# Pooled attention and a soft mixture of experts in one launch: the PE transposes of the weights leave the score banks for the bank of D^T P, by pairs of tiles

## The chip, the cores and the metric

The kernel runs on one core of one Trainium2 chip, in one launch. The metric is device time in microseconds (us), from the first to the last instruction of the program on that core and the little that lies around it. TensorE is called PE below, its weight load PEld, VectorE DVE, ScalarE ACT, GpSimd POOL, and SyncE, which issues most DMAs, SP.

## The reference, cut to what matters

```python
# attention: B=4, C=128, 12288 queries of each batch, 768 pooled keys (= values)
kv_pool = kv.reshape(B, H // 4, 4, W // 4, 4, C).mean(axis=(2, 4))
k = v = kv_pool.reshape(B, -1, C) @ w_sr
s = (q @ k.transpose(0, 2, 1)) / sqrt(C)
a = exp(s - s.max(-1)); a /= a.sum(-1) + 1e-09
x = (a @ v).reshape(B * 12288, C)
# soft MoE over all 49152 rows: 8 experts with 4 slots each = 32 columns
logits = x @ phi
d = softmax over the rows of logits;   slot_input = d.T @ x
slot_out = per expert: relu(slot_input @ w1) @ w2
c = softmax over the 32 columns of logits
return c @ slot_out
```

All inputs and the output are float32.

## The kernel before, in words

The 49152 rows are 384 tiles of 128 queries (96 tiles for each of the four batches). The program never forms x. For a tile it forms the unnormalised weights p = exp(s - max), 128 x 768, and uses them twice: the logits are p @ (v phi), divided by the row sums, and the slots need D^T P, that is (weights of the second softmax)^T @ p, which is summed over a batch and multiplied by v at the batch's end.

**A tile's steps.** `qk` (L353): six matmuls of 384 columns, for an exact product of values split into two parts, into a score tile of two PSUM banks. `top` (L357, L359): DVE's row maximum and its shift. `exp` (L369): ACT's exponential from the score tile to p in SBUF; its accumulator output, a row sum for each query, goes to a column of `SUMS`. p must then be transposed, because the logits contract over the 768 keys. Four of its six blocks of 128 keys go through the DMA: `hi` (L376, ACT) and `lo` (L379, POOL) split them into two fp16 parts, and `turn` (L384, SP) issues a transposing DMA into `pt`. The other two blocks go through PE: `tp` (L391) makes two PE transposes and `tev` (L402) is the DVE copy of the result to `pf` in SBUF. In this kernel the transposes of tile i are written to columns 384 to 511 of the two banks of the score tile of tile i+2 (`AHEAD = 2`), whose scores take columns 0 to 383 of each bank, and each tile has its own 256-column copy.

**A group's steps.** Eight tiles are a group (47 such groups, and two of four tiles at the end). `lmm` (L418) forms the group's logits from `pf` (fp32) and `pt` (fp16) in the bank `L`; `lt_out` (ACT), `lt_turn` (PE, L443), `recip` (L451, L453: the row sums plus eps, and the reciprocal), `logits`, `colmax`, `cross` (PE, L483), `newmax`, `below`, `weights` (ACT, L505) and `scaled` (L518, gives `dp`) carry the running softmax over the rows. `total_mm` (L524) and `ymm` (L541, 8 matmuls of 192 columns for a pair of tiles as the order prints them, each run as two entries of the trace: 64 for a group) accumulate the group's sum and D^T P in the bank `DB`, columns 0 to 191 and 192; `total` (L532) adds into `EA`, and `yacc` (L551) into `acc`. The row sums of the groups, `SUMS`, are columns 208 to 231 of the same bank `DB`.

**PSUM.** Eight banks: three score tiles (ring `s`) of two banks, one bank `L`, one bank `DB`. Instructions of different engines that touch one bank of a tile are made to wait for each other by semaphores even where their columns differ (two reads too); the rows of the profile that the prediction quotes show such waits.

**Order.** The program is written by a list scheduler (class `Plan`): each step is an `op` with an engine, an estimated duration, a latency, a priority, the steps that it depends on, and the rings that it takes (`acq`) or uses (`use`). `emit` picks by estimated start time and priority, and what it picks is the order of the instructions on each engine's queue; the engines then run their queues in order, each instruction waiting on its semaphores. So the numbers in `dve`, `act`, `pool` and in the `op` calls set the order and nothing else. Rings: 3 score tiles, 11 pairs of p (`p32`), 6 `hl`, 6 `pt`, 5 pairs of `pf`, one `L`, one `D`. SP carries, in order, the loads of q, the transposing DMAs and the loads of the next batch's kv, which POOL adds up (L253).

After the last tile comes the tail: the experts, the second softmax's weights c (transposed on PE into `L` and `DB` by turns, L896), and the product with the slots' outputs (L917), copied by DVE and ACT and sent out.

Of the kernel before, what the change touches and what calls it, by code (L numbers as in the profile page):

```python
# [122 lines left out]
def attention_then_soft_moe(ctx: ExitStack, tc: tile.TileContext, qT, kv0, kvT, w_sr, w_srT, phi, w1, w2, outT):  # L123
# [34 lines left out]

    KD = 4
    KP = NT - KD  # L160
    AHEAD = 2

    RINGS = {"p32": 11, "hl": 6, "pt": 6, "pf": 5, "e": 2, "q": 3, "qs": 2, "s": 3, "L": 1, "D": 1, "dp": 2, "lt": 1, "kT": 2, "U": 2, "V": 1, "kv": 1}
    plan = Plan(RINGS)
# [196 lines left out]
    def exp(i):  # L361
        g = GOF[i]
        if i == groups[g][0]:
            o = 208 + GMAX * (g % 3)
            SUMS[g] = DB[:, o : o + GMAX]
        if i % 2 == 0:
            P32[i // 2] = ring("p32", [P, 2, NK], F32, f"p_{i // 2}")
        t = i - groups[g][0]
        nc.scalar.activation(  # L369
            P32[i // 2][:, i % 2, :].rearrange("p (h k) -> p h k", h=2), S[i][:, :, :HK], AF.Exp, bias=NM.pop(i), scale=1.0,  # L370
            accum_out=SUMS[g][:, t : t + 1],
        )

# [9 lines left out]
            PT[i // 2] = ring("pt", [P, 2, 2 * KD, P], F16, f"pt_{i // 2}")  # L383
        nc.sync.dma_start_transpose(out=PT[i // 2][:, i % 2], in_=HL.pop(i).rearrange("p a k -> p (a k)"))  # L384

    def tp(i):
        if i + AHEAD >= NTL:
            S[i + AHEAD] = sslot(f"t_{i}")
        for x in range(KP):
            k = KD + x  # L390
            nc.tensor.transpose(  # L391
                out=S[i + AHEAD][:, x, HK : HK + P], in_=P32[i // 2][:, i % 2, k * P : (k + 1) * P], identity=ident
            )

    def tev(i):
        if i % 2 == 0:
            PF[i // 2] = ring("pf", [P, KP, 2, P], F32, f"pf_{i // 2}")
        dst, src = PF[i // 2][:, :, i % 2, :], S[i + AHEAD][:, :, HK : HK + P]
        if TEV(i) == "ACT":
            nc.scalar.activation(dst, src, AF.Copy)  # L400
        else:
            nc.vector.tensor_copy(dst, src)  # L402

# [185 lines left out]


    def dve(n):
        return n / 960 + 0.09

    def act(n, aps=0):
        return n / 1200 + 0.1 + 0.093 * aps

    def pool(n):
        return 0.1 + n * 1.93e-3  # L600

    HEAD = 22.0
    PER = 2.0
# [1 line left out]

    def T(i):
        return HEAD + i * PER

    def TEV(i):
        return "DVE"  # L610

    pooled[0] = stage[:, KVC - 1, :]
    ops["q", 0] = op("ACT", 0.3, 9.0, -300, [], lambda: q_load(0), acq=[("q", 0)])
# [57 lines left out]
    def group_ops(g):  # L671
        s, n = groups[g]
        b = s // TPB
        first = s % TPB == 0
        base = T(s + n - 1) + 2.0
        lk = ("L", g)
        pts = [("pt", p) for p in range(s // 2, (s + n) // 2)]
        p32 = [("p32", p) for p in range(s // 2, (s + n) // 2)]
        pfs = [("pf", p) for p in range(s // 2, (s + n) // 2)]
        k = [0]  # L680

        def go(name, eng, cost, dep, fn, acq=(), use=(), lat=0.1, raw=0.12):
            k[0] += 1
            ops[name, g] = op(eng, cost, lat, base + 0.05 * k[0], dep, fn, acq=acq, use=use, raw=raw)
            return ops[name, g]

        turns = [ops["turn", i] for i in range(s, s + n)]
        mm = 4 * KD * max(0.0255, gt(g) * P / 9000)
        a = go("l0", "PE", 4 * KP * gt(g) * P / 2200, [ops["tev", i] for i in range(s, s + n)] + [ops["u", b]], lambda: lmm(g, 0),
               acq=[lk], use=pfs + [("U", b)], lat=0.17)  # L690
        for x in range(3):
            a = go(f"l{x + 1}", "PE", mm, [a] + (turns if x == 0 else []), lambda x=x: lmm(g, x + 1), use=[lk, ("U", b)] + pts, lat=0.17, raw=0.0)
        a = go("lt", "ACT", act(gt(g) * P, 1), [a], lambda: lt_out(g), acq=[("lt", g)], use=[lk])
        a1 = go("tt", "PE", 0.14 * gt(g), [a], lambda: lt_turn(g), use=[lk, ("lt", g)], lat=0.25)
        r = go("r", "DVE", 0.38, [a, ops["e", s + n - 1]], lambda: recip(g), use=[lk])
        a = go("ll", "DVE", dve(n * NS), [a1, r], lambda: logits(g), use=[lk])
        a = go("cm", "DVE", dve(n * NS) + 0.33, [a], lambda: colmax(g), use=[lk])
        a = go("cx", "PE", 0.27, [a], lambda: cross(g), use=[lk], lat=0.3)
        rc = go("rc", "DVE", 0.18, [r], lambda: rcopy(g), use=[lk])
        a = go("nm", "DVE", 0.55, [a, ops.get(("nm", g - 1))], lambda: newmax(g), use=[lk])  # L700
        sb = go("sb", "DVE", dve(n * NS), [a], lambda: below(g), use=[lk])
        w = go("w", "ACT", act(n * NS), [sb], lambda: weights(g), acq=[("e", g)], use=[lk])
        al = go("al", "ACT", 0.29, [a], lambda: decay(g)) if g else None
        d = go("dp", "DVE", dve(n * NS), [w, rc], lambda: scaled(g), acq=[("dp", g)], use=[lk, ("e", g)])
        t = go("tm", "PE", 0.14 * n / NQD, [w], lambda: total_mm(g), acq=[("D", g)], use=[("e", g)], lat=0.3)
        y = d
        for t0 in range(0, n, 2):
            y = go(f"y{t0}", "PE", 2 * 8 * 0.0425, [y, t], lambda t0=t0: ymm(g, t0, t0 + 2), use=[("dp", g), p32[t0 // 2], ("D", g)], lat=0.2, raw=0.0)
        ya = go("ya", "DVE", dve(NT * NS), [y, t, al, ops.get(("yt", b - 1)) if first else ops["ya", g - 1]], lambda: yacc(g), use=[("D", g)])
        go("to", "DVE", 0.16, [t, al, ops.get(("to", g - 1))], lambda: total(g), use=[("D", g)])  # L710
        rm = go("rm", "DVE", dve(n * NS), [sb], lambda: rowmax(g))
        rm = go("rs", "POOL", pool(n * NS), [rm], lambda: rowsub(g))
        ops["c", g] = go("re", "ACT", act(n * NS), [rm], lambda: rowexp(g))
        if (s + n) % TPB == 0:
            ty = go("ytu", "DVE", dve(NT * NS), [ya, ops.get(("sl", b - 1))], lambda: yturn(b))
            ops["yt", b] = ty
            sl = go("sl_", "PE", 0.27 * NT, [ty, ops["v", b]], lambda: slots(b), acq=[("D", ("s", b))], use=[("V", b)], lat=0.3)
            ops["sl", b] = sl
            m = go("ms", "DVE", 0.35, [ops["nm", g], ops.get(("sa", b - 1))], lambda: mstep(b, g), use=[lk])
            if b:  # L720
                m = go("me", "ACT", 0.2, [m], lambda: mexp(b))
            ops["sa", b] = go("sa_", "DVE", 0.35, [sl, m], lambda: sacc(b), use=[("D", ("s", b))])

    qn = 3
    for i in range(NTL):
# [3 lines left out]
        if i % TB == 0:  # L729
            if iq >= 1 and iq + 2 < NB:  # L730
                ops["q", iq + 2] = op("SP", 0.75, 2.0, t - 2, [ops["ql", iq - 1], ops["q", iq + 1]], lambda n=iq + 2: q_load(n), acq=[("q", iq + 2)])
            for n in ([0, 1] if iq == 0 else [iq + 1]):
                if n < NB:
                    a = op("ACT", act(BQ), 0.1, t - 2.0 if n else -50, [ops["q", n], ops.get(("ql", n - 1))], lambda n=n: q_hi(n), acq=[("qs", n)], use=[("q", n)])
                    ops["ql", n] = op("POOL", 1.31, 0.1, t - 1.0 if n else -50, [a], lambda n=n: q_lo(n), use=[("qs", n), ("q", n)])
        kd = [ops["k", b, 0], ops["k", b, 1]]
        ops["qk", i] = op("PE", 6 * 0.163, 0.17, t, [ops["ql", iq], ops.get(("qk", i - 1))] + kd, lambda i=i: qk(i), acq=[("s", i)], use=[("qs", iq), ("kT", b)], raw=0.0)
        a = op("DVE", dve(NK) + 0.1, 0.1, t + 1, [ops["qk", i]], lambda i=i: top(i), use=[("s", i)])
        ops["e", i] = op("ACT", 0.91 + 0.06, 0.1, t + 2, [a, ops.get(("e", i - 1))], lambda i=i: exp(i), acq=[("p32", i // 2)] if i % 2 == 0 else [],
                         use=[("s", i)] + ([("p32", i // 2)] if i % 2 else []))  # L740
        a = ops["hi", i] = op("ACT", act(KD * P), 0.1, t + 4, [ops["e", i], ops.get(("hi", i - 1))], lambda i=i: hi(i), acq=[("hl", i)], use=[("p32", i // 2)], raw=0.15)
        a = op("POOL", pool(KD * P), 0.1, t + 5, [a], lambda i=i: lo(i), use=[("hl", i), ("p32", i // 2)])
        ops["turn", i] = op("SP", 1.55, 2.2, t + 6, [a, ops.get(("turn", i - 1))], lambda i=i: turn(i), acq=[("pt", i // 2)] if i % 2 == 0 else [],
                            use=[("hl", i)] + ([("pt", i // 2)] if i % 2 else []))
        pend = [i - AHEAD] if i < NTL - 1 else [i - AHEAD + x for x in range(AHEAD + 1)]
        for x in pend:
            if x < 0:
                continue
            sk = ("s", x + AHEAD)
            late = x + AHEAD >= NTL  # L750
            a = op("PE", 0.135 * KP, 0.2, T(x) + 4.5, [ops["e", x], None if late else ops["qk", x + AHEAD]], lambda x=x: tp(x), acq=[sk] if late else [],
                   use=([] if late else [sk]) + [("p32", x // 2)], raw=0.0)
            ev = TEV(x)
            ops["tev", x] = op(ev, (act if ev == "ACT" else dve)(KP * P), 0.1, T(x) + 5.0, [a, ops.get(("tev", x - 1))], lambda x=x: tev(x),
                               acq=[("pf", x // 2)] if x % 2 == 0 else [], use=[sk] + ([("pf", x // 2)] if x % 2 else []))
            ops["tev_", x] = ops["tev", x]
        for x in pend:
            if x >= 0 and x == sum(groups[GOF[x]]) - 1:
                group_ops(GOF[x])
        ib = i % TPB  # L760
        if ib == 8 and b + 1 < B:
            nb = b + 1
# [285 lines left out]
```

## Time and profile before

| | |
|---|---|
| median of 3 runs | 1283.15 us (1279.59 to 1289.29) |
| the profiled execution, its own time | 1278.79 us |
| its span, first to last instruction | 1277.0 us |
| last `qk` of the program ends | 1144.1 us after the span's start |
| busy, of the span: PE / DVE / ACT / POOL | 77% / 65% / 60% / 54% |
| mean granted TensorE clock | 0.944 |

How to read it: the profile's page gives the busy time of each engine, the costliest groups of instructions (with the mean ns of one, the idle time of the engine just before them and who ended it), and the chain that ended last. The trace behind it also gives who waited for whom, the busy time of each engine in any stretch of the span, and the instructions in order of time. A PE entry's time runs from its start to its modelled end, so two neighbours can overlap; the step from one start to the next is what an instruction really takes of the engine.

### The profile page before, as it was taken

Reading aid. Unit: us, or ns where it says so; the run is one execution under the profiler, and the core shown is the slowest. Engines: PE = TensorE matmul, PEld = TensorE weight load, DVE = VectorE, ACT = ScalarE, POOL = GpSimd, SP = SyncE. Lnnn points to the kernel's source line nnn. Section 1 sums busy time; section 2 is a strip of 40 time slices with the busy share of each in tenths; the row PEclk is TensorE's granted clock in tenths of the full one; section 3 lists DMA queues with packets and bytes.
Section 4 is the critical chain, followed back from the end, with each engine's and each line's share of the span. In section 5 each row is a group of like instructions: output and inputs, shape, how many; then the busy total and the mean of one; then the engine's idle time right before and its main releaser. Section 6 shows DMA issues by size and latency. Waiting matters only on the chain. (4 is left out here: it accounts for less than half of the span.)

```text
span 1277.0 us, 27861 instructions
## 1 busy us (share of the span) xinstructions
PE 989.5 (77%) x10392; PEld 759.8 (60%) x10392; DVE 824.8 (65%) x2085; ACT 760.9 (60%) x1567; POOL 695.6 (54%) x584
## 2 busy tenths in 40 slices
PE   2787777778877877878878777887887787876876
PEld 2665666565666656656666666666665565654454
DVE  5665675666766756666766757656666666664675
ACT  1756675566666655666666656556576666661454
POOL 1576774454577864455487855455455555541231
PEclk9999999999999989999999999989999999996765
DMA  6688775555688765565688755466566565557477
GB/s 243 131 179 174 159 143 104 98 116 105 122 191 173 167 122 104 103 118 120 144 171 165 171 124 114 88 116 117 111 123 119 104 125 109 100 99 281 173 321 297
DMA packets 433016, 186.54 MB, mean 146 GB/s; under 512 B 408561, under 2 KB 410353, under 8 KB 432881
## 3 DMA queue, kind: packets, MB, share of 16 engines
q1 hardware_dynamic: 432304, 184.35, 65.3%
q8 instruction: 82, 1.34, 0.5%
q14 instruction: 54, 0.43, 0.1%
q10 hardware_dynamic: 576, 0.41, 0.1%
HBM read 58.87 MB, written 25.17 MB: 66 GB/s over the span
## 5 line engine op out<-in xcount | busy, mean ns | idle before, releaser
L379 POOL TENSOR_TENSOR hl<-p,hl 128x512 f16<-128x512 f32 x384 | 445.1, 1163 | 379.8 <-ACT hl L376 276.5
L369 ACT ACTIVATE p<-s,nm 128x768 f32<-128x768 f32 x384 | 345.8, 900 | 383.0 <-DVE pf L402 179.1
L353 PE MATMUL s<-kT,qs 128*128 128x384 f32 x2304 | 502.7, 355 | 0.4 <-DVE pf L402 0.3
L357 DVE TENSOR_REDUCE top<-s 128x1 f32<-128x768 f32 x384 | 365.2, 951 | 48.9 <-PE s L391 28.2
L353 PEld LDWEIGHTS s<-kT,qs 128*128 128x128 f32 x2304 | 390.2, 191 | 4.9 <-issue 3.4
L541 PE MATMUL DB<-p,dp 128*32 128x192 f32 x3072 | 168.8, 360 | 105.6 <-ACT p L369 96.5
L376 ACT ACTIVATE hl<-p 128x512 f16<-128x512 f32 x384 | 239.7, 629 | 8.5
L402 DVE COPY pf<-s 128x256 f32<-128x256 f32 x382 | 159.7, 418 | 98.3 <-ACT p L369 53.8
L391 PE MATMUL s<-ident,p 128*128 128x128 f32 x764 | 155.8, 285 | 82.8 <-ACT p L369 55.2
L541 PEld LDWEIGHTS DB<-p,dp 128*32 128x32 f32 x3072 | 94.0, 118 | 169.9 <-ACT p L369 123.4
L391 PEld LDWEIGHTS s<-ident,p 128*128 128x128 f32 x764 | 92.5, 144 | 144.6 <-ACT p L369 82.1
L343 POOL TENSOR_TENSOR qs<-q,qs 128x512 fp32r<-128x512 f32 x96 | 124.2, 1294 | 75.6 <-ACT qs L340 65.5
L551 DVE SCALAR_TENSOR_TENSOR acc<-acc,al,DB 128x192 f32<-128x192 f32 x45 | 18.6, 414 | 99.8 <-PE DB L541 68.3
L340 ACT ACTIVATE qs<-q 128x512 fp32r<-128x512 f32 x96 | 60.3, 629 | 22.9 <-PE s L353 12.2
L418 PE MATMUL L<-pt,u 128*32 128x256 f16 (+1 forms) x2352 | 74.0, 274 | 0.0
L253 POOL TENSOR_TENSOR LL<-LL 128x1536 f32<-128x1536 f32 x21 | 72.9, 3471 | 0.0
L359 DVE TENSOR_SCALAR nm<-top 128x1 f32<-128x1 f32 x384 | 59.1, 154 | 16.0 <-ACT p L369 0.5
L418 PEld LDWEIGHTS <-u 128*32 128x32 f16 x2352 | 59.7, 99 | 12.3 <-issue 10.7
L369 ACT ACTIVATION_READ_ACCUMULATOR p<-s,nm 128x1 f32 x384 | 63.3, 165 | 0.0
L889 POOL TENSOR_TENSOR LL<-LL,RM 128x512 f32<-128x512 f32 x24 | 24.9, 1049 | 69.5 <-DVE RM L884 69.5
L418 PE MATMUL L<-pf,us 128*32 128x256 f32 (+1 forms) x784 | 55.5, 390 | 0.7 <-DVE pf L402 0.4
L560 POOL TENSOR_TENSOR LL<-rm,LL 128x256 f32<-128x256 f32 (+1 forms) x49 | 29.9, 610 | 45.7 <-DVE rm L556 43.6
(118 smaller groups left out, 764.2 us busy)
## 6 DMA issues: line engine op xcount, KB each, us to landing
q<-qT SPq DMA_DIRECT2D x95, 256.0 KB, 2.9
outT<-o SPq DMA_DIRECT2D x30, 768.0 KB, 4.1
LL<-kvT SPq DMA_DIRECT2D x24, 768.0 KB, 5.0
kv<-kv SPq DMA_DIRECT2D x8, 768.0 KB, 9.9
pt<-hl SPq DMA_TRANSPOSE x384, 3.1
w<-w SPq DMA_DIRECT2D x7, 768.0 KB, 9.0
w<-w SPq DMA_DIRECT2D x11, 256.0 KB, 8.7
outT<-o SPq DMA_DIRECT2D x4, 384.0 KB, 3.9
```

Of the source, the lines that this page charges most:

```text
L253: nc.gpsimd.tensor_tensor(out=stage[:, 2:4, :], in0=stage[:, 2:4, :], in1=stage[:, 0:2, :], op=ALU.add)
L340: nc.scalar.activation(QSP[i][:, 0], QS[i], AF.Copy)
L343: nc.gpsimd.tensor_tensor(out=QSP[i][:, 1], in0=QS[i], in1=QSP[i][:, 0].bitcast(F32), op=ALU.subtract)
L353: nc.tensor.matmul(s[:, h, :HK], a, k[:, m, h * HK : (h + 1) * HK], start=(n == 0), stop=(n == 2))
L357: nc.vector.tensor_reduce(out=nm, in_=S[i][:, :, :HK], axis=XY, op=ALU.max, negate=True)
L369: nc.scalar.activation(P32[i // 2][:, i % 2, :].rearrange("p (h k) -> p h k", h=2), S[i][:, :, :HK], AF.Exp, bias=NM.pop(i), scale=1.0, ac ...
L376: nc.scalar.activation(HL[i][:, 0], P32[i // 2][:, i % 2, : KD * P], AF.Copy)
L379: nc.gpsimd.tensor_tensor(out=HL[i][:, 1], in0=P32[i // 2][:, i % 2, : KD * P], in1=HL[i][:, 0], op=ALU.subtract)
L391: nc.tensor.transpose(out=S[i + AHEAD][:, x, HK : HK + P], in_=P32[i // 2][:, i % 2, k * P : (k + 1) * P], identity=ident)
L402: nc.vector.tensor_copy(dst, src)
L418: nc.tensor.matmul(out.rearrange("p (h q) -> p h q", q=P) if gt(g) == 2 else out, lhs, rhs, start=start, stop=stop)
L541: nc.tensor.matmul(G[g]["D"][j * NS : (j + 1) * NS, : NT * NS].rearrange("p (k r) -> p k r", k=NT), G[g]["dp"][:, t, :], p[:, j], start=(t ...
```

## The change

The PE transposes of a pair of tiles (four, 512 columns) are written to the bank `DB`, as a step of their own that takes the ring `D`, which the group's `total_mm` and `ymm` take too. One DVE copy of 512 columns takes the place of two of 256. The row sums move from `DB` to an SBUF tile. `AHEAD` goes, and so do the score tiles that the last two tiles' transposes took. The priorities of the transposes (t+14) and of a group's steps (16 after its last tile's time) are set later, and the estimated durations of several steps are changed. Lines that only drop comments or blanks are left out; line numbers of the changed kernel are lower: L352 for `qk`, L356 for `top`, L367 for `exp`, L389 for `tp`, L393 for `tev`, L409 for `lmm`, L515 for `total_mm`, L523 for `total`, L532 for `ymm`, L540 and L542 for `yacc`.

```diff
     def exp(i):
         g = GOF[i]
         if i == groups[g][0]:
-            o = 208 + GMAX * (g % 3)
-            SUMS[g] = DB[:, o : o + GMAX]
+            SUMS[g] = wp.tile([P, GMAX], F32, tag="sums", name=f"sums_{g}", bufs=3)
...
-    def tp(i):
-        if i + AHEAD >= NTL:
-            S[i + AHEAD] = sslot(f"t_{i}")
+    def tp(u):
         for x in range(KP):
-            k = KD + x
-            nc.tensor.transpose(
-                out=S[i + AHEAD][:, x, HK : HK + P], in_=P32[i // 2][:, i % 2, k * P : (k + 1) * P], identity=ident
-            )
-
-    def tev(i):
-        if i % 2 == 0:
-            PF[i // 2] = ring("pf", [P, KP, 2, P], F32, f"pf_{i // 2}")
-        dst, src = PF[i // 2][:, :, i % 2, :], S[i + AHEAD][:, :, HK : HK + P]
-        if TEV(i) == "ACT":
-            nc.scalar.activation(dst, src, AF.Copy)
-        else:
-            nc.vector.tensor_copy(dst, src)
+            for h in range(2):
+                k = KD + x
+                o = (2 * x + h) * P
+                nc.tensor.transpose(out=DB[:, o : o + P], in_=P32[u][:, h, k * P : (k + 1) * P], identity=ident)
+
+    def tev(u):
+        PF[u] = ring("pf", [P, KP, 2, P], F32, f"pf_{u}")
+        nc.vector.tensor_copy(PF[u].rearrange("p x h q -> p (x h q)"), DB[:, : 2 * KP * P])
...
     def dve(n):
-        return n / 960 + 0.09
+        return n / 960 + 0.06
...
-        base = T(s + n - 1) + 2.0
+        base = T(s + n - 1) + 16
...
-        ops["qk", i] = op("PE", 6 * 0.163, 0.17, t, ...)
-        a = op("DVE", dve(NK) + 0.1, 0.1, t + 1, ...)
+        ops["qk", i] = op("PE", 6 * 0.166, 0.3, t, ...)
+        a = op("DVE", 1.08, 0.09, t + 1, ...)
...
-        pend = [i - AHEAD] if i < NTL - 1 else [i - AHEAD + x for x in range(AHEAD + 1)]
-        for x in pend:
...
-            sk = ("s", x + AHEAD)
-            late = x + AHEAD >= NTL
-            a = op("PE", 0.135 * KP, 0.2, T(x) + 4.5, [ops["e", x], None if late else ops["qk", x + AHEAD]], lambda x=x: tp(x), acq=[sk] if late else [],
-                   use=([] if late else [sk]) + [("p32", x // 2)], raw=0.0)
-            ev = TEV(x)
-            ops["tev", x] = op(ev, (act if ev == "ACT" else dve)(KP * P), 0.1, T(x) + 5.0, [a, ops.get(("tev", x - 1))], lambda x=x: tev(x),
-                               acq=[("pf", x // 2)] if x % 2 == 0 else [], use=[sk] + ([("pf", x // 2)] if x % 2 else []))
+        if i % 2:
+            u = i // 2
+            dk = ("D", ("t", u))
+            a = op("PE", 0.135 * 2 * KP, 0.27, t + 14, [ops["e", i]], lambda u=u: tp(u), acq=[dk], use=[("p32", u)], raw=0.0)
+            ops["tev", u] = op("DVE", dve(2 * KP * P), 0.08, t + 9.0, [a, ops.get(("tev", u - 1))], lambda u=u: tev(u), acq=[("pf", u)], use=[dk])
```

What this does to PE's queue is shown at the group 24 (tiles 192 to 199, pairs p_96 to p_99), from the group's sum to the tiles after its D^T P. In a row, s_206 is the score tile of tile 206, p_102 the weights of the pair 204 and 205, e_24 and dp_24 the group's weights. Before:

```order
L353 MATMUL s_206_7787<-kT_2_6277,qs_51_7500 128x384 x6
L391 MATMUL s_206_7787<-ident_71,p_102_7760 128x128 x2
L524 MATMUL DB_97<-ones_77,e_24_7806 128x1 x2
L353 MATMUL s_207_7818<-kT_2_6277,qs_51_7500 128x384 x6
L541 MATMUL DB_97<-p_96_7292,dp_24_7816 32x192 x8
L541 MATMUL DB_97<-p_97_7349,dp_24_7816 32x192 x8
L541 MATMUL DB_97<-p_98_7446,dp_24_7816 32x192 x8
L541 MATMUL DB_97<-p_99_7514,dp_24_7816 32x192 x8
L391 MATMUL s_207_7818<-ident_71,p_102_7760 128x128 x2
L353 MATMUL s_208_7884<-kT_2_6277,qs_52_7715 128x384 x6
```

And in the changed kernel:

```order
L352 MATMUL s_211_7790<-kT_2_6202,qs_52_7509 128x384 x6
L389 MATMUL DB_97<-ident_71,p_102_7596 128x128 x4
L352 MATMUL s_212_7818<-kT_2_6202,qs_53_7676 128x384 x6
L515 MATMUL DB_97<-ones_77,e_24_7816 128x1 x2
L532 MATMUL DB_97<-p_96_7180,dp_24_7833 32x192 x8
L532 MATMUL DB_97<-p_97_7261,dp_24_7833 32x192 x8
L532 MATMUL DB_97<-p_98_7309,dp_24_7833 32x192 x8
L532 MATMUL DB_97<-p_99_7354,dp_24_7833 32x192 x8
L352 MATMUL s_213_7895<-kT_2_6202,qs_53_7676 128x384 x6
L389 MATMUL DB_97<-ident_71,p_103_7661 128x128 x4
L352 MATMUL s_214_7916<-kT_2_6202,qs_53_7676 128x384 x6
```

The transposes of tiles 204 and 205 now stand behind the scores of tile 211 instead of behind those of 206 and 207, four at a time, and group 24's D^T P stands five tiles later, with a `qk` between it and the next use of the bank on either side. In the waits that the order lists, 67 rows of `ymm` waited on ACT before and none do now; 233 rows of `tp` waited on ACT before and none do now.

DVE's queue at the same place in the changed kernel, from the copy of the pair 102 to the copy of D^T P:

```order
L393 COPY pf_102_7826<-DB_97 128x512
L509 TENSOR_TENSOR dp_24_7833<-e_24_7816,L_24_7667 128x256
L356 TENSOR_REDUCE top_210_7839<-s_210_7775 128x1
L358 TENSOR_SCALAR nm_210_7841<-top_210_7839 128x1
L523 SCALAR_TENSOR_TENSOR EA_92<-EA_92,al_24_7828,DB_97 128x1
L356 TENSOR_REDUCE top_211_7863<-s_211_7790 128x1
L358 TENSOR_SCALAR nm_211_7865<-top_211_7863 128x1
L356 TENSOR_REDUCE top_212_7888<-s_212_7818 128x1
L358 TENSOR_SCALAR nm_212_7890<-top_212_7888 128x1
L540 COPY acc_89<-DB_97 128x192
```

Before, the same stretch held two 256-column copies from the score tiles between the maxima; now the only copies are those from `DB`, and the add into `EA` stands behind one maximum. In the changed kernel the third pair's `ymm` (p_98) waits on DVE for that add.

At the end of the program, 383 being the last tile, the changed PE queue has the logits of the group 46 behind the last `qk`; before they stood ahead of it.

More of the change, by code (lines that the diff above doesn't have):

```diff
@@ L160, in attention_then_soft_moe @@
     KP = NT - KD
-    AHEAD = 2
     RINGS = {"p32": 11, "hl": 6, "pt": 6, "pf": 5, "e": 2, "q": 3, "qs": 2, "s": 3, "L": 1, "D": 1, "dp": 2, "lt": 1, "kT": 2, "U": 2, "V": 1, "kv": 1}
@@ L369, in exp @@
         nc.scalar.activation(
-            P32[i // 2][:, i % 2, :].rearrange("p (h k) -> p h k", h=2), S[i][:, :, :HK], AF.Exp, bias=NM.pop(i), scale=1.0,
+            P32[i // 2][:, i % 2, :].rearrange("p (h k) -> p h k", h=2), S.pop(i)[:, :, :HK], AF.Exp, bias=NM.pop(i), scale=1.0,
             accum_out=SUMS[g][:, t : t + 1],
@@ L593, in dve @@
     def dve(n):
-        return n / 960 + 0.09
+        return n / 960 + 0.06
     def act(n, aps=0):
-        return n / 1200 + 0.1 + 0.093 * aps
+        return n / 1000 + 0.03 + 0.09 * aps
     def pool(n):
-        return 0.1 + n * 1.93e-3
+        return 0.04 + n * 2.13e-3
     HEAD = 22.0
@@ L607, in T @@
         return HEAD + i * PER
-    def TEV(i):
-        return "DVE"
     pooled[0] = stage[:, KVC - 1, :]
@@ L688, in group_ops @@
         mm = 4 * KD * max(0.0255, gt(g) * P / 9000)
-        a = go("l0", "PE", 4 * KP * gt(g) * P / 2200, [ops["tev", i] for i in range(s, s + n)] + [ops["u", b]], lambda: lmm(g, 0),
+        a = go("l0", "PE", 4 * KP * gt(g) * P / 2200, [ops["tev", u] for u in range(s // 2, (s + n) // 2)] + [ops["u", b]], lambda: lmm(g, 0),
                acq=[lk], use=pfs + [("U", b)], lat=0.17)
@@ L734, in attention_then_soft_moe @@
                     a = op("ACT", act(BQ), 0.1, t - 2.0 if n else -50, [ops["q", n], ops.get(("ql", n - 1))], lambda n=n: q_hi(n), acq=[("qs", n)], use=[("q", n)])
-                    ops["ql", n] = op("POOL", 1.31, 0.1, t - 1.0 if n else -50, [a], lambda n=n: q_lo(n), use=[("qs", n), ("q", n)])
+                    ops["ql", n] = op("POOL", 1.25, 0.04, t - 1.0 if n else -50, [a], lambda n=n: q_lo(n), use=[("qs", n), ("q", n)])
         kd = [ops["k", b, 0], ops["k", b, 1]]
-        ops["qk", i] = op("PE", 6 * 0.163, 0.17, t, [ops["ql", iq], ops.get(("qk", i - 1))] + kd, lambda i=i: qk(i), acq=[("s", i)], use=[("qs", iq), ("kT", b)], raw=0.0)
-        a = op("DVE", dve(NK) + 0.1, 0.1, t + 1, [ops["qk", i]], lambda i=i: top(i), use=[("s", i)])
-        ops["e", i] = op("ACT", 0.91 + 0.06, 0.1, t + 2, [a, ops.get(("e", i - 1))], lambda i=i: exp(i), acq=[("p32", i // 2)] if i % 2 == 0 else [],
+        ops["qk", i] = op("PE", 6 * 0.166, 0.3, t, [ops["ql", iq], ops.get(("qk", i - 1))] + kd, lambda i=i: qk(i), acq=[("s", i)], use=[("qs", iq), ("kT", b)], raw=0.0)
+        a = op("DVE", 1.08, 0.09, t + 1, [ops["qk", i]], lambda i=i: top(i), use=[("s", i)])
+        ops["e", i] = op("ACT", 0.94, 0.04, t + 2, [a, ops.get(("e", i - 1))], lambda i=i: exp(i), acq=[("p32", i // 2)] if i % 2 == 0 else [],
                          use=[("s", i)] + ([("p32", i // 2)] if i % 2 else []))
@@ L744, in attention_then_soft_moe @@
                             use=[("hl", i)] + ([("pt", i // 2)] if i % 2 else []))
-        pend = [i - AHEAD] if i < NTL - 1 else [i - AHEAD + x for x in range(AHEAD + 1)]
-        for x in pend:
-            if x < 0:
-                continue
-            sk = ("s", x + AHEAD)
-            late = x + AHEAD >= NTL
-            a = op("PE", 0.135 * KP, 0.2, T(x) + 4.5, [ops["e", x], None if late else ops["qk", x + AHEAD]], lambda x=x: tp(x), acq=[sk] if late else [],
-                   use=([] if late else [sk]) + [("p32", x // 2)], raw=0.0)
-            ev = TEV(x)
-            ops["tev", x] = op(ev, (act if ev == "ACT" else dve)(KP * P), 0.1, T(x) + 5.0, [a, ops.get(("tev", x - 1))], lambda x=x: tev(x),
-                               acq=[("pf", x // 2)] if x % 2 == 0 else [], use=[sk] + ([("pf", x // 2)] if x % 2 else []))
[L756 to L759, printed above, removed]
+        if i % 2:
[3 more added lines that the diff above has]
+            ops["tev", u] = op("DVE", dve(2 * KP * P), 0.08, t + 9.0, [a, ops.get(("tev", u - 1))], lambda u=u: tev(u), acq=[("pf", u)], use=[dk])
+        g = GOF[i]
+        if i == groups[g][0] + groups[g][1] - 1:
+            group_ops(g)
         ib = i % TPB
```

## Prediction

> **What bounds the kernel now.** I read the page first, then the engines' busy time in the stage of the 384 tiles, then who waits for whom there, then one place in order of time. The stage, and the tail behind it, from the view of stretches:
>
> ```profile
> core 0: us, PE busy (x) PEld busy (x) DVE busy (x) ACT busy (x) POOL busy (x), PEclk, DMA share, GB/s
> 22.40:1144.10 1121.70, 889.91 (x9542) 698.55 (x9542) 728.61 (x1890) 702.25 (x1453) 662.23 (x546) 0.98 0.65 129
> 1144.10:1277.00 132.90, 97.36 (x846) 60.28 (x846) 82.48 (x182) 55.51 (x110) 29.81 (x30) 0.64 0.68 261
> ```
>
> The stage takes 1121.7 of the 1277.0 us, 2.92 us for each of its 384 tiles. PE is the busiest engine, 890 us or 79%; DVE has 65%, ACT 63%, POOL 59%, the DMA engines 0.65. No engine is full; PE's 232 idle us are waits, and the view of waits of this stretch names them:
>
> ```profile
> ACT p L369 <- DVE pf L402: 175.6, 128, 4.2
> PE DB L541 <- ACT p L369: 94.7, 66, 2.1
> ACT p L369 <- PE s L391: 71.7, 57, 3.3
> ACT p L369 <- PE DB L541: 70.6, 46, 3.8
> PE s L391 <- ACT p L369: 55.2, 62, 1.8
> PE L L443 <- DVE r L453: 22.6, 22, 1.1
> DVE L L451 <- ACT p L369: 22.0, 20, 1.2
> PE s L391 <- DVE top L357: 19.4, 21, 1.5
> PE DB L541 <- DVE EA L532: 8.1, 9, 1.3
> ```
>
> D^T P (L541) needs nothing that a current exp (L369) makes: its p is from an earlier group. It waits because each exp writes a row sum to the same bank, DB. In the same way an exp needs nothing from the copy pf (L402) of the tile two before; that copy reads the banks whose scores the exp reads. How the two make each other late is seen in order of time at one group's D^T P (rows of other instructions left out):
>
> ```profile
> 660.13 0.61 PE L524 MATMUL DB<-ones,e 128*128 128x1 f32 x4
> ...
> 661.82 0.86 PE L541 MATMUL DB<-p,dp 128*32 128x192 f32 x16
> ...
> 662.82 0.21 DVE L532 SCALAR_TENSOR_TENSOR EA<-EA,al,DB 128x1 f32<-128x1 f32 x1 [1.12 <-PE DB L541]
> 662.95 0.42 DVE L402 COPY pf<-s 128x256 f32<-128x256 f32 x1
> ...
> 663.46 0.90 ACT L369 ACTIVATE p<-s,nm 128x768 f32<-128x768 f32 x1 [2.33 <-DVE pf L402]
> ...
> 664.48 2.16 PE L541 MATMUL DB<-p,dp 128*32 128x192 f32 x48 [1.79 <-ACT p L369]
> ...
> 666.70 0.90 ACT L369 ACTIVATE p<-s,nm 128x768 f32<-128x768 f32 x1 [1.62 <-PE DB L541]
> ...
> 667.70 0.41 DVE L551 SCALAR_TENSOR_TENSOR acc<-acc,al,DB 128x192 f32<-128x192 f32 x1 [1.90 <-ACT p L369]
> ```
>
> The first 16 matmuls end, DVE reads the bank and makes a copy, the exp that waited 2.33 us for that copy runs, the other 48 matmuls wait 1.79 us for the exp, the next exp waits 1.62 us for them, and the copy of D^T P waits 1.90 us for that exp. D^T P is 0.86 + 2.16 = 3.02 us of work and keeps PE from 661.82 to 666.64.
>
> **What PE would take without waits.** From the steps from start to start near the stage's end:
>
> ```profile
> 1133.20 1.07 PE L418 MATMUL L<-pf,us 128*32 128x256 f32 x16
> ...
> 1134.52 1.30 PE L353 MATMUL s<-kT,qs 128*128 128x384 f32 x6
> 1135.66 0.38 PE L391 MATMUL s<-ident,p 128*128 128x128 f32 x2
> 1135.79 1.30 PE L353 MATMUL s<-kT,qs 128*128 128x384 f32 x6
> 1137.02 1.50 PE L418 MATMUL L<-pt,u 128*32 128x256 f16 x48
> ...
> 1141.14 0.41 PE L443 MATMUL L<-ident,lt 128*128 128x128 f32 x2 [1.06 <-DVE r L453]
> ...
> 1142.81 1.29 PE L353 MATMUL s<-kT,qs 128*128 128x384 f32 x6
> 1144.24 0.39 PE L483 MATMUL L<-cq,sel 128*128 128x4 f32 x2
> ```
>
> A tile's scores take PE 1.14 us before the next instruction starts (1134.52 to 1135.66), two transposes 0.13, together 1.27. A group of eight tiles is 8 x 1.27 + 1.07 + 1.50 (logits) + 0.61 (sum) + 3.02 (D^T P) + 0.41 + 0.39 = 17.2 us, 2.15 a tile, against 2.92 measured. So a stage near 2.2 us a tile is the most that any order could give, and what the change is worth lies in how much of the 232 idle us it returns.
>
> **What it removes.** No exp writes to DB any more, so D^T P doesn't wait for exps: 94.7 us. The transposes (L391) no longer write into a score tile, so they wait neither for the maximum that reads it (19.4) nor, set eight tiles behind their exp by the order shown above, for the exp (55.2). recip (L451) reads its sums from SBUF and no longer waits 22.0 us for exps, by which the 22.6 us of L443 behind it go; this is the least sure, since both also touch the bank L (0 to 22.6; I take all, as the two rows match). Sum: 94.7 + 55.2 + 19.4 + 22.6 = 191.9 us of PE. The 175.6 + 71.7 + 70.6 us that exps wait go with them; they are the other side of the same ping-pong, and I don't count them again.
>
> **What it adds.** The instructions, by rows of the view of groups over the whole span:
>
> ```profile
> L357 DVE TENSOR_REDUCE top<-s 128x1 f32<-128x768 f32 x384 | 365.2, 951 | 48.9 <-PE s L391 28.2 <-PE s L353 19.0
> L369 ACT ACTIVATION_READ_ACCUMULATOR p<-s,nm 128x1 f32 x384 | 63.3, 165 | 0.0
> L402 DVE COPY pf<-s 128x256 f32<-128x256 f32 x382 | 159.7, 418 | 98.3 <-ACT p L369 53.8 <-PE s L391 31.0 <-ACT hl L376 12.7
> L926 DVE COPY o<-po 128x768 f32<-128x768 f32 x32 | 30.4, 950 | 10.5 <-PE po L917 9.8
> L509 ACT ACTIVATE al<-c,c 128x1 f32<-128x1 f32 x48 | 13.8, 287 | 6.0 <-DVE c L490 6.0
> ```
>
> A copy of 512 columns lies between 418 ns (256) and 950 ns (768): 418 + 256 x (950 - 418)/512 = 684 ns. 192 of them take 131 us where the 384 took 160: DVE gains 29 us, which at 65% busy is worth nothing by itself. PE's transposes stay as many. The row sum written to SBUF may cost ACT from 0 to 0.12 us more (287 ns for a whole one-column ACT instruction into SBUF, less 165): at most 47 us on an engine with 420 idle us, so I take 0.
>
> The Trainium skill ("ScalarE: Activation LUTs", Step-by-step: what each stage is for) says that ACT reaches PSUM sooner than SBUF, which speaks against moving the sums; no run shows the two side by side, it gives no figure, and by it the sum would move by less than the bound just given.
>
> The new cost is the bank. Per group DB is handed over five times: a transposed pair to its copy, four times, and D^T P to acc. The next user of the bank on PE must wait for a DVE instruction: 0.68 us (0.41 for acc), some 0.06 us on either side, and whatever DVE is in the middle of, at worst a maximum with its shift, 0.95 + 0.15. That is 0.8 to 1.9 us; the one qk that the order puts between covers 1.14. So a handover costs from 0 to 0.76 us of PE. I take 0.1, because DVE is free or in short instructions a good part of the time: 5 x 47 groups x 0.1 = 24 us. The add into EA stands behind a maximum and its shift (some 1.2 us with the gaps), while the half of D^T P ahead of it takes 1.5; then 0.21 and two handoffs: 0.33 us a group, 15 us, of which 8.1 are there today: 7 us.
>
> Queued behind a waiting PE instruction are the next qk's, and behind those top and exp. The other new wait is theirs: qk of tile i takes the score tile of i-3 and waits for its exp. qk, top and exp of one tile are 1.3 + 1.1 + 0.9 and three handoffs, 3.6 us, against three tiles' time of 7.6, so 4 us are spare; the group's chain on DVE (L468 to L497, some 2 us in a piece) takes from that. 0 to 2.0 us a group; I take 0.4, since the spare is the larger: 19 us. Last, a group's logits move behind the last qk: 2.57 us and part of the small steps, 6 us more behind the stage, taken whole.
>
> **The sum.** -191.9 + 24 + 7 + 19 + 6 = -136, from the profiled 1278.8 us to 1143. The median of the runs shown is 4.4 us above the profiled execution, so the forecast for a median is 1147 us, 10.6% below 1283.15. The head and the tail stay otherwise.
>
> The Trainium skill ("PSUM — Partial Sum Buffer", PSUM bank collisions raise a hardware error) has the rule behind all this: two engines may not be in one bank and quadrant at once, whatever the columns, reads included, so programs guard by the bank. The trace agrees: 175.6 us of exps behind a copy that only reads the same bank. By the rule the transposes and D^T P must now exclude each other's readers in full; that is the 0 to 0.76 us above, and it is what the first rival is made of.
>
> **Rivals.**
>
> Slower: DB as the new bottleneck. If DVE starts each copy only after a whole maximum, a handover costs the whole 0.76 us, 5 x 47 x 0.76 = 179 us, and the time is 1283.15 - 191.9 + 179 + 32 = 1302 us. It is the case from 0.68 us a handover on ((191.9 - 32)/235). For it: in DVE's order maxima stand right ahead of copies. Against: a qk stands between nearly all handovers, and two stand behind the transposes of p_103, which cover even 1.9 us.
>
> Same: the waits of exps and transposes hang on something that the change leaves, such as the old p that the new one overwrites; then the gain is eaten. For it: many exps still carry a wait on PE. Against: the place shown above, where each wait is of the bank.
>
> Smaller gain: the wait moves to the score tiles. If the chain on DVE costs the full 2.0 us a group, 94 instead of 19, the time is 1147 + 75 = 1222. Near it lies the DMA: its share is higher where the next batch's kv is loaded,
>
> ```profile
> 500.00:600.00 100.00, 80.62 (x856) 62.97 (x854) 65.80 (x174) 64.60 (x136) 52.92 (x47) 0.98 0.60 114
> 620.00:720.00 100.00, 79.64 (x866) 63.57 (x858) 65.89 (x168) 64.06 (x133) 71.08 (x54) 1.00 0.79 167
> ```
>
> 0.79 there, though PE is no less busy. At the forecast pace it would be 0.79 x 1122/980 = 0.90, POOL 0.81: not full. If it did bind in those stretches, some four tenths of the stage, the gain there would go: 1147 + 0.4 x 136 = 1201.
>
> Larger gain: nothing of the new waits shows and PE's other waits (232 - 192 = 40 us) halve: 1283.15 - 191.9 - 20 + 6 = 1077.
>
> **How the numbers follow.** The forecast's case, 1100 to 1200: 0.50. Larger gain: 0.15. Smaller gain, 1200 to 1270: 0.19. Same: 0.06. Slower: 0.10. Within 1% is about what a measurement of this kernel can tell from no change. So faster by over 1%: 0.84, same 0.06, slower 0.10. The range goes from below the larger gain's 1077 to above the smaller gain's 1222: 1070 to 1240.
>
> **What would show it.** Right: in the stage, no waits of D^T P for p and none of p for the copy pf; PE near 0.90 busy; some 2.55 us a tile; the copies near 0.68 us; D^T P of a group within 4 us. PE's waits for the copy pf or for acc below 40 us in sum. Wrong: such waits of over 160 us (the slower rival), qk waiting over 90 us for exps (the smaller gain), exps that still wait for PE or DVE by 300 us (same), a DMA share near 1 under kv loads, or a last qk later than 1060 us.

## The result and the profile after

The changed kernel takes 1089.7 us (median of 4 runs, 1089.19 to 1091.37) against 1281.37 us before (4 runs): the ratio is 0.8496, 95% interval 0.8458 to 0.8535. The forecast was 1147 with a range of 1070 to 1240; the measured time lies in the range, but below the likeliest case (1100 to 1200), near the number of the case called "larger gain" (1077).

The page's first lines and the view of stretches, split at the end of the last qk (953.6 us; before 1144.1), with the same columns as before:

```profile
span 1089.6 us, 27676 instructions
PE 963.6 (88%) x10392; PEld 772.4 (71%) x10392; DVE 799.1 (73%) x1893; ACT 756.4 (69%) x1567; POOL 692.1 (64%) x584
```

```profile
22.40:953.60 931.20, 862.40 (x9469) 710.09 (x9472) 701.16 (x1694) 697.70 (x1451) 657.91 (x546) 0.99 0.83 155
953.60:1089.60 136.00, 98.91 (x922) 61.35 (x922) 84.11 (x186) 55.62 (x111) 30.21 (x31) 0.67 0.69 258
```

The stage of the tiles went from 1121.7 to 931.2 us, 2.43 us a tile; what lies behind it from 132.9 to 136.0. PE's idle time in the stage fell from 231.8 to 68.8 us and its busy time from 889.9 to 862.4. What PE still waits for there, from the view of waits:

```profile
PE s L352 <- ACT p L367: 25.9, 42, 0.8
PE DB L532 <- DVE EA L523: 18.1, 45, 0.4
...
PE DB L515 <- ACT e L496: 4.2, 3, 1.4
PE DB L389 <- DVE pf L393: 3.7, 4, 1.1
PE DB L515 <- DVE pf L393: 0.6, 3, 0.2
...
PE L L434 <- DVE r L444: 0.2, 1, 0.2
```

All four waits that the prediction took away are gone but for 0.2 us (94.7, 55.2, 19.4 and 22.6 us before). Two remain of any size: qk behind the exp that frees its score tile, and the second half of D^T P behind DVE's read of the sum. In order of time, at one group's D^T P (rows of other instructions left out):

```profile
828.96 0.50 PE L515 MATMUL DB<-ones,e 128*128 128x1 f32 x4
...
829.39 1.51 PE L532 MATMUL DB<-p,dp 128*32 128x192 f32 x32
...
831.03 0.21 DVE L523 SCALAR_TENSOR_TENSOR EA<-EA,al,DB 128x1 f32<-128x1 f32 x1 [1.06 <-ACT p L367]
...
831.30 1.51 PE L532 MATMUL DB<-p,dp 128*32 128x192 f32 x32 [0.41 <-DVE EA L523]
...
832.74 1.31 PE L352 MATMUL s<-kT,qs 128*128 128x384 f32 x6
...
833.27 0.41 DVE L542 SCALAR_TENSOR_TENSOR acc<-acc,al,DB 128x192 f32<-128x192 f32 x1
...
833.89 0.60 PE L389 MATMUL DB<-ident,p 128*128 128x128 f32 x4
```

From its start to the next instruction's, D^T P now keeps PE for 3.35 us (829.39 to 832.74) where it was 4.6 in the stretch shown of before (661.82 to the logits that follow at 666.45); the copy into acc lies under the next qk, and the transposes behind that qk wait for nothing. The rows of two other costs that the prediction bounded, from the view of groups:

```profile
L393 DVE COPY pf<-DB 128x512 f32<-128x512 f32 x192 | 131.4, 684 | 66.2 <-PE DB L389 66.2
L367 ACT ACTIVATION_READ_ACCUMULATOR p<-s,nm 128x1 f32 x384 | 74.2, 193 | 0.0
```

### The profile page after: what moved, and what is told of

Its sections match the earlier page's. It is cut to its first block, busy times and chain, and to the rows that moved or that the text cites. A ratio compares the mean times of both kernels' runs of the same rounds, so it can differ in the third digit from the quotient of the medians.

```text
span 1089.6 us, 27676 instructions
## 1 busy us (share of the span) xinstructions
PE 963.6 (88%) x10392; PEld 772.4 (71%) x10392; DVE 799.1 (73%) x1893; ACT 756.4 (69%) x1567; POOL 692.1 (64%) x584
## 5 line engine op out<-in xcount | busy, mean ns | idle before, releaser
L352 PE MATMUL s<-kT,qs 128*128 128x384 f32 x2304 | 489.5, 352 | 26.0 <-ACT p L367 25.9
L367 ACT ACTIVATE p<-s,nm 128x768 f32<-128x768 f32 x384 | 345.0, 899 | 189.8 <-DVE L L480 112.9
L352 PEld LDWEIGHTS s<-kT,qs 128*128 128x128 f32 x2304 | 389.8, 189 | 59.1 <-ACT p L367 41.2
L356 DVE TENSOR_REDUCE top<-s 128x1 f32<-128x768 f32 x384 | 364.7, 950 | 33.0 <-PE s L352 32.7
L393 DVE COPY pf<-DB 128x512 f32<-128x512 f32 x192 | 131.4, 684 | 66.2 <-PE DB L389 66.2
L532 PE MATMUL DB<-p,dp 128*32 128x192 f32 x3072 | 154.1, 343 | 19.1 <-DVE EA L523 18.8
L342 POOL TENSOR_TENSOR qs<-q,qs 128x512 fp32r<-128x512 f32 x96 | 125.1, 1303 | 29.8 <-ACT qs L339 18.1
L532 PEld LDWEIGHTS DB<-p,dp 128*32 128x32 f32 x3072 | 93.2, 113 | 60.4 <-DVE EA L523 37.0
L389 PE MATMUL DB<-ident,p 128*128 128x128 f32 x768 | 118.2, 276 | 4.1 <-DVE pf L393 4.1
L389 PEld LDWEIGHTS DB<-ident,p 128*128 128x128 f32 x768 | 91.7, 141 | 19.9 <-issue 10.2
L409 PE MATMUL L<-pt,u 128*32 128x256 f16 (+1 forms) x2352 | 81.8, 273 | 0.0
L409 PEld LDWEIGHTS <-u 128*32 128x32 f16 x2352 | 68.3, 97 | 9.9 <-issue 1.8
L367 ACT ACTIVATION_READ_ACCUMULATOR p<-s,nm 128x1 f32 x384 | 74.2, 193 | 0.0
L409 PE MATMUL L<-pf,us 128*32 128x256 f32 (+1 forms) x784 | 66.7, 386 | 2.1
L870 POOL TENSOR_TENSOR LL<-LL,RM 128x512 f32<-128x512 f32 x24 | 25.0, 1049 | 67.2 <-DVE RM L865 67.2
L898 PE MATMUL po<-c,shl 32*128 32x384 f32 x384 | 40.9, 507 | 13.1 <-DVE o L907 10.2
```

Of the source, the lines that this page charges most:

```text
L342: nc.gpsimd.tensor_tensor(out=QSP[i][:, 1], in0=QS[i], in1=QSP[i][:, 0].bitcast(F32), op=ALU.subtract)
L352: nc.tensor.matmul(s[:, h, :HK], a, k[:, m, h * HK : (h + 1) * HK], start=(n == 0), stop=(n == 2))
L356: nc.vector.tensor_reduce(out=nm, in_=S[i][:, :, :HK], axis=XY, op=ALU.max, negate=True)
L367: nc.scalar.activation(P32[i // 2][:, i % 2, :].rearrange("p (h k) -> p h k", h=2), S.pop(i)[:, :, :HK], AF.Exp, bias=NM.pop(i), scale=1.0 ...
L389: nc.tensor.transpose(out=DB[:, o : o + P], in_=P32[u][:, h, k * P : (k + 1) * P], identity=ident)
L393: nc.vector.tensor_copy(PF[u].rearrange("p x h q -> p (x h q)"), DB[:, : 2 * KP * P])
```

## The experiments

Two theories stood against each other at first: that the shared banks held PE, or that the new durations and priorities, which set only the order, made the gain. Ratios are to the kernel before, run beside each, with their 95% interval.

**The sums alone.** The scheduler doesn't see where the sums lie, so the order is that of the kernel before, instruction by instruction.

```diff
-            o = 208 + GMAX * (g % 3)
-            SUMS[g] = DB[:, o : o + GMAX]
+            SUMS[g] = wp.tile([P, GMAX], F32, tag="sums", name=f"sums_{g}", bufs=3)
```

> The kernel before with one part of the change: the row sums in SBUF, all else as before. If the shared banks held PE (my theory), the 94.7 us that D^T P waited for exps and the 22 us of the recip's path go: about 1283 - 117 = 1166 us, between 1150 and 1205, and the rows of D^T P waiting for p are gone, while exps still wait for the copy pf by 100 us or more. If the new order (durations and priorities) made the gain, this stays above 1255.

1158.6 us, ratio 0.904 (0.9017 to 0.9063). From its view of waits in the stage:

```profile
ACT p L368 <- DVE pf L401: 170.9, 129, 4.0
...
PE s L390 <- ACT p L368: 55.2, 65, 1.8
...
ACT p L368 <- PE s L390: 42.7, 48, 3.6
```

D^T P no longer waits for p at all, and the 70.6 us that exps waited for D^T P are gone. Around the score banks, exps wait for the copy pf and transposes for exps as before (175.6 and 55.2 us then); exps wait less for transposes (71.7 then). 123 us came from where 24 columns lie, with the order unchanged: the cost of the shared bank DB is shown. The stage, with the same columns as before:

```profile
22.40:1028.10 1005.70, 871.58 (x9542) 696.88 (x9542) 727.38 (x1890) 706.34 (x1452) 661.19 (x546) 0.99 0.76 143
```

PE's idle time fell by 97.7 us (231.8 to 134.1), not by the 117 expected: PE now waits 15.7 us for the add into EA (8.1 before) and 27.3 for the maxima (19.4 before), and 6.3 of the 22.6 us behind recip remain. The rest of the 123 us is mostly PE's busy time, which fell by 18.3.

**The durations alone**, in the kernel before (the lines for ACT, POOL, the maximum, the exp and q's low part, changed in the same way, are left out):

```diff
-        return n / 960 + 0.09
+        return n / 960 + 0.06
...
-        ops["qk", i] = op("PE", 6 * 0.163, 0.17, t, ...)
+        ops["qk", i] = op("PE", 6 * 0.166, 0.3, t, ...)
```

> The kernel before with the changed kernel's estimated durations (of dve, act, pool, qk, top, exp, q's low part) and nothing else: only the order can differ. If the shared banks held PE, the waits stay and the time is within 25 us of 1281. If the order made the gain, it falls by 95 us or more, to 1186 or less.

1262.6 us, ratio 0.9868 (0.9816 to 0.9921): 19 us, inside the first theory's bound. Over the whole run D^T P still waits 101.2 us for p (96.5 before).

**The changed kernel with the old durations**, that is with all these lines put back:

> The changed kernel with the estimated durations of the kernel before. If the shared banks held PE, it keeps most of the gain: 1090 to 1135. If the order made the gain, it goes back above 1185.

1070.1 us, ratio 0.8358 (0.8327 to 0.8389): faster than the changed kernel by 20 us. The new durations are not the source of the gain; together with the rest they cost something. PE's idle time in the stage is the same, 68.6 us against 68.8; what is shorter is its busy time, 842.1 us against 862.4.

**Only the banks**: the old durations and the old priorities too (the copy pf keeps its priority of t+9, where it was 5 before).

```diff
-            a = op("PE", 0.135 * 2 * KP, 0.27, t + 14, ...)
+            a = op("PE", 0.135 * 2 * KP, 0.27, t + 4.5, ...)
...
-        base = T(s + n - 1) + 16
+        base = T(s + n - 1) + 2.0
```

> The changed kernel with both the estimated durations and the priorities of the kernel before: only the banks differ from before (sums in SBUF, transposes by pairs in DB). If the banks made the gain, it lies within 30 us of the changed kernel's 1090. If the later priorities (transposes behind older tiles, groups later) are needed to keep PE from waiting for exps, it lies at 1130 or above, with PE's transposes waiting for exps by 30 us or more.

1127.3 us, ratio 0.881 (0.8764 to 0.8856). Between the two bounds: a little outside the 30 us, a little short of 1130. And the same two lines with the new durations kept:

> The changed kernel with only the priorities of the kernel before (transposes at t+4.5, groups at 2 after the last tile), its new durations kept. If the priorities carry part of the gain, the 55 us of transposes waiting for exps come back and it lies above 1125. If not, it stays within 20 us of 1090.

1131.7 us, ratio 0.8832 (0.8777 to 0.8887). So the priorities carry 42 us with the new durations and 57 us with the old ones. But not as I had expected: the transposes hardly wait for exps in either (0.5 and 0.2 us). The banks-only kernel's largest wait of PE is another:

```profile
PE s L352 <- ACT p L367: 69.8, 49, 2.7
PE DB L532 <- DVE EA L523: 15.6, 45, 0.4
PE DB L389 <- DVE pf L393: 11.5, 27, 0.6
```

qk waits for the exp of three tiles before, 69.8 us against 25.9 in the changed kernel and 6.2 in the one with old durations. Why these exps come later under the old priorities was not tried apart.

**The sums back in DB**, in the changed kernel. Since a pair's transposes fill the bank, they go tile by tile:

```diff
-            SUMS[g] = wp.tile([P, GMAX], F32, tag="sums", name=f"sums_{g}", bufs=3)
+            o = 208 + GMAX * (g % 3)
+            SUMS[g] = DB[:, o : o + GMAX]
...
+    def tp(i):
+        for x in range(KP):
+            k = KD + x
+            o = 256 + x * P
+            nc.tensor.transpose(out=DB[:, o : o + P], in_=P32[i // 2][:, i % 2, k * P : (k + 1) * P], identity=ident)
...
+        nc.vector.tensor_copy(PF[i // 2][:, :, i % 2, :], DB[:, 256:512].rearrange("p (x q) -> p x q", q=P))
```

> The changed kernel with the row sums back in columns 208 to 231 of DB; to make room the transposes go tile by tile (two, 256 columns) into columns 256 to 511 of DB, with a copy of 256 each. Every exp now shares a bank with D^T P and with the transposes. If the shared bank is what costs, this is over 100 us above the changed kernel, 1190 or more. If what matters is that the score banks are free of transposes, it stays below 1140.

1453.8 us, ratio 1.1355 (1.1309 to 1.1402). At the end of its order the last group's sums take columns of group 45's before these are read; that touches values, not times. Its control has the same order, and the sums in SBUF (in four buffers, because of that overlap):

> The changed kernel with the transposes tile by tile (two, 256 columns, into columns 256 to 511 of DB, with a copy of 256 each), the row sums in SBUF (four buffers): the control of x4_sums_in_DB, with the same order and only the place of the sums different. If the sums' bank made x4's 1454 us, this lies below 1200, within 100 us of the changed kernel. If it is the eight handovers of DB a group instead of four, it lies above 1300.

1271.3 us, ratio 0.9918 (0.9889 to 0.9946): between the two bounds, so neither theory alone holds. Both parts are large. The place of the sums is worth 1454 - 1271 = 182 us here; and by single tiles the changed kernel loses 182 us too (1271 against 1090). The waits on PE with the sums in DB, then without:

```profile
PE DB L389 <- ACT p L368: 81.8, 124, 1.3
PE DB L389 <- DVE pf L394: 71.6, 70, 2.0
PE DB L533 <- ACT p L368: 53.2, 47, 1.4
```

```profile
PE DB L388 <- DVE pf L393: 55.6, 46, 2.0
PE DB L515 <- DVE pf L393: 36.4, 36, 2.4
PE s L352 <- ACT p L367: 27.5, 44, 1.8
PE DB L532 <- DVE EA L523: 15.3, 44, 0.4
```

The second table is the slower rival's mechanism: DB handed over by way of a late copy. PE's timeline of that control shows where, at one group:

```profile
720.00 0.38 PE L388 MATMUL DB<-ident,p 128*128 128x128 f32 x2
720.72 0.39 PE L474 MATMUL L<-cq,sel 128*128 128x4 f32 x2 [0.34 <-DVE cq L471]
723.09 0.69 PE L388 MATMUL DB<-ident,p 128*128 128x128 f32 x2 [1.99 <-DVE pf L393]
724.39 0.98 PE L515 MATMUL DB<-ones,e 128*128 128x1 f32 x4 [0.61 <-DVE pf L393]
725.30 1.50 PE L532 MATMUL DB<-p,dp 128*32 128x192 f32 x16
727.15 3.13 PE L532 MATMUL DB<-p,dp 128*32 128x192 f32 x48 [0.34 <-DVE EA L523]
730.21 1.34 PE L352 MATMUL s<-kT,qs 128*128 128x384 f32 x6
```

Between the first two pairs of transposes stands one small matmul and no qk, and DVE comes to the copy only after a maximum, its shift and four steps of the group's chain: 1.99 us. Then the sum waits 0.61 us more. And after these idle microseconds D^T P, 3.0 us elsewhere, takes 1.50 + 3.13 us, because TensorE's clock was cut to half: it is 1.00 from 718.70 to 722.10 and 0.52 from there to 729.00. The view of wider stretches around it (granted clock in the last column but two):

```profile
709.00:724.00 15.00, 11.65 (x117) 9.30 (x115) 11.43 (x32) 9.53 (x20) 12.89 (x9) 0.94 0.46 107
724.00:733.00 9.00, 8.27 (x85) 6.12 (x86) 3.27 (x9) 5.43 (x12) 5.70 (x6) 0.71 0.50 118
```

So the 182 us of the single tiles are not handovers alone. In the stage PE's idle time rose by 91 us against the changed kernel (68.8 to 159.9) and its busy time by 73 (862.4 to 935.2), with 225 us at half clock against 10; the part behind the stage took the other 18.

**The remaining wait of D^T P.** The add into EA is placed behind the copy of D^T P:

```diff
-        go("to", "DVE", 0.16, [t, al, ops.get(("to", g - 1))], lambda: total(g), use=[("D", g)])
+        go("to", "DVE", 0.16, [ya, t, al, ops.get(("to", g - 1))], lambda: total(g), use=[("D", g)])
```

> The changed kernel with the add into EA placed behind the copy of D^T P, so that the second half of D^T P no longer waits for that DVE read of DB (18 us of PE's waits in the changed kernel's profile). If PE's waits set the stage's length one for one, the time falls by 10 to 18 us, to 1072 to 1080. If DVE's order behind the maxima sets it, the wait moves elsewhere and the time stays within 5 us of 1090.

1056.3 us, ratio 0.8259 (0.8219 to 0.8298): 33 us less than the changed kernel, more than the 18 us of the wait and outside both bounds. D^T P is one stretch now:

```profile
824.61 0.50 PE L515 MATMUL DB<-ones,e 128*128 128x1 f32 x4
825.04 2.81 PE L532 MATMUL DB<-p,dp 128*32 128x192 f32 x64
```

The wait of 0.41 us had more behind it: in the changed kernel's chain of one group, EA stood between ACT's work and PE's, and the copy pf that the logits need came so late that their last matmuls waited too (the fp32 half took 1.54 us there at 838.03, here 1.07). The order around it moved as well, so the 33 us are not the wait's alone: PE's idle time in the stage fell by 13 us (to 55.9), its busy time by 18 (to 844.1). With the old durations:

> The kernel with the old durations (1070 us in its run) with the add into EA placed behind the copy of D^T P. If PE's waits set the length, it falls by 10 to 17 us, to 1053 to 1060. If not, it stays within 5 us of 1070.

1047.1 us, ratio 0.8173 (0.8123 to 0.8223), the best of all and 6 us below the bound. Last, that kernel with two of PE's durations as the trace has them:

```diff
-        ops["qk", i] = op("PE", 6 * 0.163, 0.17, t, ...)
+        ops["qk", i] = op("PE", 1.14, 0.16, t, ...)
...
-            y = go(f"y{t0}", "PE", 2 * 8 * 0.0425, ...)
+            y = go(f"y{t0}", "PE", 0.75, ...)
```

> The kernel x9 (old durations, total last, 1047 us) with two durations set to the steps of PE from start to start that the trace shows: 1.14 us for the scores of a tile and 0.75 us for the D^T P of a pair. If the scheduler's order was limited by wrong durations of PE, the time falls by 8 us or more, below 1039. If its order is good by chance rather than by accurate durations, it moves either way by up to 25 us.

1069.1 us, ratio 0.8336 (0.8293 to 0.8378): 22 us slower. Two durations nearer to the trace made a worse order here. PE's waits don't show it, since its idle time in the stage is 62.8 us against 67.2; its busy time is 848.9 us against 825.0.

## Why the prediction was right, and where its sum was off

**What bounds and what goes: right.** The four waits of 191.9 us are gone in the profile, and the first experiment, in an unchanged order, returns 123 us where the terms for the sums were 94.7 + 22.6 = 117. That the two numbers are so near is in part luck: only 97.7 us of it are idle time.

**The handovers of DB: mis-sized.** I charged 24 us (0.1 us each); the rows say 3.7 + 0.6 = 4.3. In this order one qk covers the copy nearly always. It is not the banks alone that decide this: in the same kernel with the old durations the handovers cost PE 23.9 + 8.2 = 32.1 us, near the charge. That the mechanism is real, and costs even more than the 0.76 us at which I ended, is shown by the control with single tiles: 1.99 us for one without cover, and the half clock on top.

**The add into EA:** 7 us more were charged, 18.1 - 8.1 = 10 measured as PE's wait. The new place in the order, which was the reason given, is not needed for most of it: the first experiment has 15.7 us of this wait in the old order. The run that removes the wait returns 33 us, with an order that moved; a wait's own length doesn't say what hangs on it.

**The score tiles:** 19 us charged, 25.9 measured. **The end:** 6 charged, 136.0 - 132.9 = 3.1 measured.

**What the sum left out.** It ran over waits by name and stopped there. Of PE's 163.0 us less idle time the named terms, as measured, make -191.9 + 4.3 + 10 + 25.9 = -151.7; 11.3 more came from small waits. And PE's busy time, which I held fixed, fell by 27.5 us. Part of that is the clock: its record in the trace has 47.8 us at half rate in the stage before and 10.2 after, and 37.6 us less at half rate saves PE up to 19 us. I had the granted clock of 0.98 in the first row that I quoted, and didn't ask what made it fall; the last section shows after what stretches it does. Some 2.6 us are the logits of one group, which now run behind the stage. The closer row of four transposes is probably a small part: in the first experiment, with the transposes as before, the busy time had already fallen by 18.3 us and the time at half rate to 17.1 us. The exact shares stay open. In all, the profiled execution became 187.4 us shorter where the sum had 136. Of the 51 us between, 27.5 are this busy time, 11.3 the small waits and 12.7 the new costs (43.3 us measured, 56 charged).

**The floor that I didn't weigh enough.** The floor of 2.15 us a tile stood in the text, and PE's work without waits was the better guide: 2.43 is 1.13 times it. The rival "larger gain" (1077) had a chance of 0.15, and its number came near for another reason than it gave: the new waits do show, 40 us of them, and the busy time, which it left alone, fell.

**The DMA.** One sign of being wrong appeared without its cause. A DMA share near 1 under kv loads was to show that the DMA binds. In the changed kernel the share is 1.11 from 294 to 348 us and 1.01 from 510 to 564 (the view sums the times of packets, so it can pass 1). Yet all waits of the engines for a DMA in the stage make 6.6 us: the share alone doesn't say that it binds.

**Parts that the prediction didn't separate.** Against the kernel before, the banks alone give 153 us (1127), the priorities 57 more (1070), and the new durations take 20 back (1090). That the priorities spare the transposes' wait for exps was my reason for counting the 55.2 us; in the experiments the wait didn't come back, so the bank move alone had already removed it. Why the order from the new durations is worse stays open in part. As PE's idle time is the same, the 20 us lie in its busy time, and a row of PE can hold a wait of its weight loads, as the logits of 1.54 us above did: in the changed kernel the weight loads of the logits wait 13.1 us for the copy pf, and with the old durations no such wait is listed. Besides, in the changed kernel exps wait in most groups for the maximum behind the group's chain on DVE,

```profile
ACT p L367 <- DVE L L480: 112.9, 39, 3.7
ACT p L367 <- DVE nm L358: 59.3, 98, 2.4
```

(a maximum's shift ends just ahead of L480), but the kernel with the one change of EA, at 1056 us, has nearly the same wait (105.1 us).

The Trainium skill ("PSUM — Partial Sum Buffer", PSUM bank collisions raise a hardware error) asks that two engines be kept apart by the bank and quadrant, or more simply by the bank, whatever the columns; the experiment with the sums back in DB, where 24 columns that nobody else touches cost 182 us, is what that looks like in time.

## What to carry to other kernels

Before moving work between engines, look in the view of waits for pairs that share no data, only a bank: where a small result lies can cost more than what computes it. When two users must share a bank, put enough of other work between them on the waiting engine's queue to cover the reader in full, and batch the handovers; half as many, with the order and the full clock that came with them, were worth 182 us here. Give a scheduler several sets of plausible durations and measure: three sets that differ by a tenth or two of a microsecond gave 1047, 1056 and 1069 us with the sum last, and the set with two durations from the trace was not the best. Where the waits of two kernels are alike, compare the busy time of the engine and its granted clock too.

## What the runs showed of the hardware that was not expected

The row-sum step of an exp takes 165 ns into PSUM (164 in the run with the sums back in DB) and 193 to 195 ns into SBUF, in every run: 28 ns, 11 us of ACT over 384 tiles, inside the bound of 0 to 0.12 us. The Trainium skill ("ScalarE: Activation LUTs", Step-by-step: what each stage is for) says that PSUM is the nearer for ACT; the runs agree and give the size.

TensorE's granted clock falls to half after stretches in which PE isn't wholly idle: in the group of the single-tile control shown above it falls at about 722.4 us, while PE waits for the copy; the transposes at 723.09 already take 0.69 us where the pair before took 0.38. In the 3.41 us ahead of the fall PE was busy for 1.82 us, with scores, a pair of transposes and one small matmul. The clock's record has 41 such falls in that stage, and PE was busy for 1.1 to 2.3 of the 3.41 us ahead of each. The Trainium skill ("TensorE: Matmul & The Clock Gate", Part 1: The HAM clock gate) gives an idle window of about 3.4 us as the condition; here stretches of that length that were not idle, but half worked, came ahead of the falls. Over the stage this left a mean clock of 0.90, and D^T P of the group shown at 4.6 instead of 3.0 us.
